# A gated mix of two linear-attention blocks: the gate weights on GpSimd's DMA queue, their transpose moved ahead of x's first block, and one weight load cut in two

## The chip, the core and the metric

The kernel runs on one core of a Trainium2 chip. The metric is the device time in microseconds of one execution; for the kernel before it is the median of three runs, 183.4 us. One further execution was taken by the hardware profiler; its own time was 183.47 us, of which 181.8 us lie between the first and the last instruction (the span). All durations below come from that execution.

The engines are named as in the profile: PE is TensorE (matmuls), PEld its weight loads, DVE is VectorE, ACT is ScalarE, POOL is GpSimd and SP is SyncE, which issues most of the DMAs. A row that ends in "q" after the engine's name (SPq, ACTq, POOLq) is an instruction of that engine's sequencer, such as the issue of a DMA.

## What is computed

One input x of 2048 rows and 640 columns goes through two attention blocks A and B that have weights of their own, and a gate mixes the two results row by row:

```python
x = A_x
g = sigmoid((x * gate_w).sum(-1, keepdims=True))       # gate_w: 640 values
def block(x, wqkv, wo):                                # 32 heads of 20 columns
    q, k, v = split(x @ wqkv)
    phi = lambda t: where(t > 0, t + 1, exp(t)) + 1e-6
    pq, pk = phi(q), phi(k)
    kv = einsum("bhsd,bhse->bhde", pk, v)
    z = einsum("bhsd->bhd", pk)
    num = einsum("bhqd,bhde->bhqe", pq, kv)
    den = einsum("bhqd,bhd->bhq", pq, z)[..., None] + 1e-6
    return heads_together(num / den) @ wo
return g * block(x, A_wqkv, A_wo) + (1 - g) * block(x, B_wqkv, B_wo)
```

## The kernel before

**Tiling.** The 2048 rows of x are 16 chunks of 128 rows; four chunks make a block of 512 rows. The 640 columns are five slabs of 128 (`DT` = 5, index c). Matmuls contract over the columns of x, so x is needed transposed: `xT` holds slab c in its partitions. For x's first block of four chunks, PE transposes the natural rows `xn` (line 250, five transposes of 128x128 a chunk, one for each slab) and DVE copies the result from PSUM to `xT` in two pieces of two and three slabs (line 253). The other three blocks are transposed by the DMA engines (line 172, fifteen DMAs on SP's queue).

**Order.** The body of the program stands in a manually scheduled region: each engine executes its instructions in the order in which the Python code emits them, and waits only for what it reads or overwrites. The stages are: the K projection of A with the gate logits (`k_first`, `k_chunk`), A's Q projection, A's products G = xT times pk and M, then the same for B interleaved with A's late work, then the outer products and the output. What matters here is the start and one load in the middle.

**The loads at the start (lines 157 to 174).** x's first four chunks (`load_x`, 160 KB each) and A's K weights (`load_wk`: slabs 0, 1 and 2 of 160 KB each, then slabs 3 and 4 together, 320 KB) are spread over SP's and ACT's queues. In the order of the code: x chunk 0 on SP, x chunk 1 on ACT, K slab 0 on SP, K slab 1 on ACT, the gate weights `g5` on SP (line 161; five rows of 128 values, 1.2 KB), x chunk 2 on ACT, K slab 2 on SP, x chunk 3 on ACT, K slabs 3 and 4 on SP. Behind them SP issues A's Q weights (line 169, three DMAs) and the fifteen DMA transposes. The framework gives the DMAs of SP and ACT eight completion semaphores in turn; the ninth such DMA uses the first one's semaphore again, and its issuing queue waits until the first has landed. In the kernel before, the ninth is the load of K slabs 3 and 4 on SP; it waits for x chunk 1.

**POOL at the start (lines 177 to 201).** POOL first builds the identity `ident` (a memset and an affine select), which the transposes on PE use, and between and after that the masks and helper matrices `maskE`, `I4`, `spread`, `E4` (a half of the tile `zE`) and a float32 identity in the memory of `GT`.

**The first matmuls.** Seven matmuls on constants (lines 207 to 209) into the PSUM tile `warm_raw` keep PE busy until x arrives. Then `k_first` (line 316) runs:

```python
x_transpose(0, 3)
x_transpose(1, 1)
gate_column(warm_raw)
pts += [ps("kA", 2), ps("kA", 3)]
for hf in range(2):
    for i in range(2):
        part(i, (0, 1), (hf,))
x_transpose(2, 0)
```

`x_transpose(i, slot)` issues the five transposes and two copies of chunk i. `gate_column` (line 220) transposes `g5` on PE into five columns of `warm_raw`'s PSUM slot, and ACT copies them (line 225, three copies) into column 640 of `wk[0]`, A's K weights. So each K matmul of the second half (`hf` = 1) has 321 columns rather than 320, and its last column is the gate's logit. `part(i, (0, 1), (hf,))` is two matmuls of chunk i with slabs 0 and 1 (line 295). The first four K matmuls have `hf` = 0 and do not read the gate column; the next four do.

**The load in the middle.** `Masks` (line 1020) runs A's product `kv_mm` with the V weights of A on PE, and then issues the load of B's V weights, `wvB` (line 1025, 800 KB, through `load_w`, line 864), which takes the memory of A's V weights. `wvB` is first read by the second `kv_mm`, at the first K-V product of B (line 1063).

Of the kernel before, what the change touches and what calls it, by code (L numbers as in the profile page):

```python
# [9 lines left out]
P = 128  # L10
# [7 lines left out]
DT = D // P  # L18
# [15 lines left out]
def kernel(  # L34
# [11 lines left out]
    nc = tc.nc  # L46
# [29 lines left out]
    def ps_raw(name, slot=None):  # L76

        if slot is None:
            slot = turn[0]
            turn[0] = (slot + 1) % 4  # L80
        return pools.get(slot, pools["ps"]).tile([P, 4 * HB], BF16, tag=f"ps{slot}", name=name)
# [5 lines left out]
    def ps(name, slot=None):  # L87

        return banks(ps_raw(name, slot))
# [20 lines left out]
    g5 = persist.tile([DT, P], BF16, name="g5")  # L110
# [37 lines left out]
    wv = [None, None]  # L148
    wq = [None, None]
    wk[0] = wpool.tile([P, DT, D + 2], BF16, tag="wk", name="wkA")  # L150
    def load_x(eng, lo, hi):
        eng.dma_start(out=xn[:, lo:hi, :], in_=xb0[:, lo:hi, :])

    def load_wk(eng, lo, hi):
        eng.dma_start(out=wk[0][:, lo:hi, 0:D], in_=wq_dram[0][:, lo:hi, D:2 * D])

    load_x(nc.sync, 0, 1)
    load_x(nc.scalar, 1, 2)
    load_wk(nc.sync, 0, 1)
    load_wk(nc.scalar, 1, 2)  # L160
    nc.sync.dma_start(out=g5[:], in_=gate_w.rearrange("(c p) -> c p", p=P))
    load_x(nc.scalar, 2, 3)
    load_wk(nc.sync, 2, 3)
    load_x(nc.scalar, 3, 4)
# [5 lines left out]
    for n in range(1, NB):  # L170
        for c in range(DT):
            nc.sync.dma_start_transpose(
                out=xT[:, c, n * HB:(n + 1) * HB], in_=x2[n * HB:(n + 1) * HB, c * P:(c + 1) * P]
# [4 lines left out]
    for r in range(4):  # L178
# [3 lines left out]
        out=spread[:].rearrange("p (h t) -> p h t", t=TW), in_=I4[:, :, None].to_broadcast([P, H, TW])  # L182
    )
    nc.gpsimd.memset(maskE[:], 1.0)
    for lo in range(0, HF, K6):
        part = maskE[:, lo:min(lo + K6, HF)]
        for sign, base in ((1, 0), (-1, Dh - 1)):
            nc.gpsimd.affine_select(
                out=part, in_=part, pattern=[[-sign * Dh, part.shape[1] // Dh], [0, Dh]],
# [3 lines left out]
    for rows, n in ((slice(0, 2 * H), H // 2), (slice(2 * H, P), H)):  # L193
        nc.gpsimd.tensor_copy(
            out=E4_rows[rows, 0:n], in_=I4[rows, 0:n, None].to_broadcast([rows.stop - rows.start, n, Dh])
# [9 lines left out]
    warm_raw = ps_raw("warm", 0)  # L205
# [14 lines left out]
    def gate_column(pt):  # L220

        at = slice(4 * HB - 2 * P, 4 * HB - 2 * P + DT)
        nc.tensor.transpose(out=pt[:, at], in_=g5[:], identity=ident[0:DT, 0:DT])
        for lo, hi in ((0, 1), (1, 2), (2, DT)):
            nc.scalar.copy(out=wk[0][:, lo:hi, D:D + 1], in_=pt[:, at, None][:, lo:hi])
# [21 lines left out]
    def x_transpose(i, slot):  # L247
        pt = ps_raw("xt", slot)
        for c in range(DT):
            nc.tensor.transpose(out=pt[:, c * P:(c + 1) * P], in_=xn[:, i, c * P:(c + 1) * P], identity=ident[:])  # L250
        src = pt[:, 0:D].rearrange("p (c n) -> p c n", c=DT)
        for lo, hi in ((0, 2), (2, DT)):
            nc.vector.tensor_copy(out=xT[:, lo:hi, i * P:(i + 1) * P], in_=src[:, lo:hi])  # L253

    class Phi:

        def __init__(self, dst, src, lifted=False):
            self.dst, self.src, self.lifted = dst, src, lifted
            e = work.tile([P] + list(dst.shape[1:]), BF16, tag="e", name="e", bufs=4)
            self.e = e[:]  # L260
            self.parts = parts = [(self.e, dst, src)] if not isinstance(src, list) else [
                (self.e[:, n], dst[:, n], part) for n, part in enumerate(src)]
            for to, lifted_to, part in parts:
                nc.scalar.activation(out=to, in_=part, func=ACT.Exp)  # L264
                if lifted is True:
                    self.lift(lifted_to, part)
# [26 lines left out]
    def k_mm(b, i, c, pt, hf):  # L293
        n = HF + (b == 0 and hf == 1)
        nc.tensor.matmul(  # L295
            pt[:, hf, 0:n], lhsT=xT[:, c, i * P:(i + 1) * P], rhs=wk[b][:, c, hf * HF:hf * HF + n],
            start=(c == 0), stop=(c == DT - 1),
        )

    def k_done(b, i, pt, lifted=False, between=None):  # L300
        f = Phi(pk[:, i, :].rearrange("p (b n) -> p b n", b=2), pt[:, :, 0:HF], lifted)
        if b == 0:
            nc.scalar.activation(out=gl[:, i:i + 1], in_=pt[:, 1, HF:HF + 1], func=ACT.Exp)
        f.clamp()
        if between is not None:
            between()
        f.top()

    def k_chunk(b, i, slot=None, lifted=False, between=None):
        pt = ps(f"k{'AB'[b]}", slot)  # L310
        for hf in range(2):
            for c in range(DT):
                k_mm(b, i, c, pt, hf)
        k_done(b, i, pt, lifted, between)

    def k_first():

        pts = []

        def part(i, cs, hfs=(0, 1)):  # L320
            for c in cs:
                for hf in hfs:
                    k_mm(0, i, c, pts[i], hf)

        x_transpose(0, 3)
        x_transpose(1, 1)
        gate_column(warm_raw)
        pts += [ps("kA", 2), ps("kA", 3)]
        for hf in range(2):
            for i in range(2):  # L330
# [3 lines that stand above are left out]
            part(i, (2,))  # L334
        x_transpose(3, 1)
        pts.append(ps("kA", 0))
        part(2, (0, 1, 2))
        for i in range(3):
            part(i, (3, 4))
            k_done(0, i, pts[i])  # L340
        k_chunk(0, 3, 1)
# [281 lines left out]
    def kv_mm(b, banks, gs, cs=range(DT)):  # L623

        for g in gs:
            hf, n = g // 3, rows_in(g)
            part = slice(blocks[g].start - hf * HF, blocks[g].stop - hf * HF)
            for k, c in enumerate(cs):
                nc.tensor.matmul(
                    banks[hf][:n, part], lhsT=wv[b][:, c, blocks[g]], rhs=GT[hf][:, c, part],  # L630
                    start=(k == 0), stop=(k == DT - 1),
                )
# [46 lines left out]
    def cells(pt):  # L679
        return [pt[:, hf] for hf in range(2)]  # L680
# [183 lines left out]
    def load_w(b, which, eng, cuts=(0, DT)):  # L864
        lo = {"q": 0, "k": D, "v": 2 * D}[which]
        t = wpool.tile([P, DT, D], BF16, tag="w" + which, name=f"w{which}{'AB'[b]}")
        for c0, c1 in zip(cuts, cuts[1:]):
            eng.dma_start(out=t[:, c0:c1], in_=wq_dram[b][:, c0:c1, lo:lo + D])
        return t
# [76 lines left out]

    with tc.manual_schedule():
        k_first()
        turn[0] = 2
        for n in range(2):  # L950
# [8 lines left out]
        for n in range(1, NB):  # L959
            nc.sync.dma_start(  # L960
                out=xn[:, n * CB:(n + 1) * CB, :], in_=x2[n * HB:(n + 1) * HB, :].rearrange("(q p) d -> p q d", p=P)
# [58 lines left out]
        class Masks:  # L1020

            def __init__(self, slot):
                self.pt = ps("kvA", slot)
                kv_mm(0, cells(self.pt), (0, 1, 2, 3, 5, 4))
                wv[1] = load_w(1, "v", nc.sync)

            def clamp(self):
                kv_mask(0, cells(self.pt), 0, 2)
# [97 lines left out]
        for i in range(1, half):  # L1126
            p, after = pairs[i], pairs[i + 1] if i + 1 < half else None
# [49 lines left out]
```

## Time and profile before

| | |
|---|---|
| median of 3 runs (lowest, highest) | 183.4 us (183.33, 183.84) |
| profiled execution: time, span | 183.47 us, 181.8 us |
| PE busy | 177.5 us |
| DVE, ACT, POOL busy | 148.2, 108.2, 5.5 us |
| DMA moved | 18.85 MB |

In the profile a row of the timeline is "start, duration, engine, line, operation, out<-in, count", and the bracket names how long the engine had been idle before it and who ended that. A PE row's duration is longer than the time to the next one's start, since matmuls are pipelined; for a group of equal matmuls the pitch is (duration of the group minus duration of one) divided by the count less one. The DMA view gives for each issue its size and the time from the start of the issue to the landing. A row of the windows view gives the busy time of each engine in a stretch, the granted clock of PE, the busy share of the DMA engines, and the GB/s.

### The profile page before, as it was taken

What the parts mean: (1) busy time and instruction counts of PE and PEld (TensorE: products, weight loads), DVE (VectorE), ACT (ScalarE), POOL (GpSimd) and SP (SyncE); (2) the same over time, 40 slices, a digit from 0 to 9 for tenths busy, and PEclk for the clock granted to TensorE, in tenths of its full rate; (3) what the DMA queues carried; (4) which work ended last, traced back from release to release, by engine and by line L of the source; (5) the groups of instructions that cost most, each with busy time, mean ns of one, the idle gap of its engine ahead of it and who ended that gap; (6) DMA issues with size and microseconds to landing.
All of it is one profiled execution on the core that took longest, in us unless ns stands there. A gap on an engine that the chain in (4) does not pass through costs nothing.

```text
span 181.8 us, 3375 instructions
## 1 busy us (share of the span) xinstructions
PE 177.5 (98%) x1275; PEld 118.8 (65%) x1285; DVE 148.2 (82%) x267; ACT 108.2 (60%) x210; POOL 5.5 (3%) x23
## 2 busy tenths in 40 slices
PE   7999999999999999999999999999999999999993
PEld 3766656655666677676666665766678777777772
DVE  0478988999999796799898987997988988686764
ACT  2066579976884512785868696964814755466210
POOL 8300000000000000000000000000000000000000
PEclk9999999999999999999999999999999999999999
DMA  5996449984108133005000000053901470222132
GB/s 180 290 177 82 98 103 272 362 176 132 51 4 235 65 116 119 0 0 180 4 2 0 0 4 2 8 149 79 291 17 28 158 180 0 108 88 97 72 130 90
DMA packets 21519, 18.85 MB, mean 104 GB/s; under 512 B 9183, under 2 KB 20991, under 8 KB 21503
## 3 DMA queue, kind: packets, MB, share of 16 engines
q1 hardware_dynamic: 20638, 17.82, 36.1%
q10 hardware_dynamic: 864, 0.82, 1.5%
q8 instruction: 10, 0.16, 0.4%
q14 instruction: 7, 0.05, 0.1%
HBM read 11.86 MB, written 4.80 MB: 92 GB/s over the span
## 4 chain that ended last, share of the span: by engine, by line
PE 96%; DMA 2%; DVE 1%; issue 0%
PE gs L515 17%; PE kA L295 12%; PE kB L295 12%; PE q L413 11%; PE qA L348 7%; PE oy L762 6%; PE oz L762 5%; PE ox L762 4%; PE ow L762 4%; PE q L348 2%; PE gB L485 2%; PE gA L485 2%; DMA xn<-in_A_x_dram 2%; PE qB L348 1%; PE xt L250 1%; PE mA L645 1%
## 5 line engine op out<-in xcount | busy, mean ns | idle before, releaser
L295 PEld LDWEIGHTS <-xT 128*128 128x128 bf16 x320 | 31.1, 98 | 15.0 <-DVE xT L253 0.2
L272 DVE TENSOR_SCALAR e<-e 128x640 bf16<-128x640 bf16 (+2 forms) x58 | 19.6, 339 | 5.8 <-ACT e L264 5.2
L295 PE MATMUL kB<-wkB,xT 128*128 128x320 bf16 x160 | 24.2, 299 | 0.0
L295 PE MATMUL kA<-wkA,xT 128*128 128x320 bf16 (+1 forms) x160 | 23.4, 301 | 0.1
L264 ACT ACTIVATE e<-q 128x512 bf16<-128x512 f32 x26 | 15.7, 603 | 5.0 <-PE q L413 3.9
L515 PEld LDWEIGHTS <-xn 128*128 128x128 bf16 x128 | 12.2, 98 | 6.0 <-issue 1.3
L264 ACT ACTIVATE e<-kB 128x640 bf16<-128x640 f32 x16 | 11.4, 710 | 7.5 <-PE kB L295 7.3
L264 ACT ACTIVATE e<-kA 128x640 bf16<-128x640 f32 x16 | 11.3, 713 | 7.6 <-PE kA L295 7.5
L348 PE MATMUL qA<-xT,wqA 128*128 128x512 bf16 x57 | 13.3, 379 | 0.2
L348 PEld LDWEIGHTS <-wqA 128*128 128x128 bf16 x64 | 7.5, 117 | 5.9
L283 DVE SCALAR_TENSOR_TENSOR pk<-kB,e 128x640 bf16<-128x640 f32 x12 | 9.9, 823 | 1.0
L825 ACT COPY u<-ox 128x320 f32<-128x320 f32 x8 | 3.4, 425 | 11.4 <-PE ox L762 11.4
L762 PEld LDWEIGHTS <-xT 128*128 128x128 bf16 x85 | 8.1, 98 | 2.9
L762 PEld LDWEIGHTS <-pqTA 128*128 128x128 bf16 x85 | 8.1, 98 | 2.8
L767 DVE TENSOR_TENSOR osb<-oz,u 128x320 bf16<-128x320 f32 (+2 forms) x18 | 8.0, 454 | 2.2 <-PE oz L762 1.8
L762 PEld LDWEIGHTS <-pqTB 128*128 128x128 bf16 x80 | 7.8, 98 | 3.0
L515 PE MATMUL gs<-pk,xn 128*128 128x320 bf16 x64 | 9.4, 299 | 0.0
L283 DVE SCALAR_TENSOR_TENSOR pk<-kA,e 128x640 bf16<-128x640 f32 x10 | 8.2, 823 | 0.9
L431 DVE TENSOR_TENSOR q<-q,p 128x512 f32<-128x512 f32 x12 | 8.3, 692 | 0.8 <-PE q L413 0.6
L264 ACT ACTIVATE e<-qA 128x1024 bf16<-128x1024 f32 x6 | 6.2, 1027 | 4.2 <-PE qA L348 3.9
L485 PEld LDWEIGHTS <-xn 128*128 128x128 bf16 x64 | 6.3, 98 | 3.0
L515 PEld LDWEIGHTS <-S 128*128 128x128 bf16 x64 | 6.0, 98 | 2.5 <-issue 0.3
(187 smaller groups left out, 348.2 us busy)
## 6 DMA issues: line engine op xcount, KB each, us to landing
out_dram<-osb SPq DMA_DIRECT2D x14, 160.0 KB, 1.8
xn<-in_A_x_dram SPq DMA_DIRECT2D x3, 640.0 KB, 5.7
wvA<-in_A_wqkv_dram SPq DMA_DIRECT2D x1, 800.0 KB, 10.5
wkB<-in_B_wqkv_dram SPq DMA_DIRECT2D x1, 800.0 KB, 4.7
wqB<-in_B_wqkv_dram SPq DMA_DIRECT2D x1, 800.0 KB, 6.4
wvB<-in_B_wqkv_dram SPq DMA_DIRECT2D x1, 800.0 KB, 4.7
MA<-m_rows SPq DMA_DIRECT2D x1, 800.0 KB, 5.1
MB<-m_rows SPq DMA_DIRECT2D x2, 400.0 KB, 4.2
```

The costliest lines, as they stand in the source:

```text
L264: nc.scalar.activation(out=to, in_=part, func=ACT.Exp)
L272: nc.vector.tensor_scalar(self.e, self.e, 1.0, EPS, op0=ALU.min, op1=ALU.add)
L283: nc.vector.scalar_tensor_tensor(out=dst, in0=src, scalar=1.0 + EPS, in1=e, op0=ALU.add, op1=ALU.max)
L295: nc.tensor.matmul(pt[:, hf, 0:n], lhsT=xT[:, c, i * P:(i + 1) * P], rhs=wk[b][:, c, hf * HF:hf * HF + n], start=(c == 0), stop=(c == DT - 1),
L348: nc.tensor.matmul(dst, lhsT=mixed(wq[b][:, c, :], m), rhs=xT[:, c, n * HB:(n + 1) * HB], start=first, stop=last,)
L413: nc.tensor.matmul(dst, lhsT=left(c), rhs=right(c), start=first and k == 0, stop=k == len(cs) - 1, skip_group_check=not first,)
L431: nc.vector.tensor_tensor(out=dst, in0=src, in1=sb, op=ALU.add)
L485: nc.tensor.matmul(pt[:, hf, 0:HF], lhsT=xn[:, i, c * P:(c + 1) * P], rhs=pk[:, i, hf * HF:(hf + 1) * HF], start=(i == 0), stop=(i == ST - 1),
L515: nc.tensor.matmul(pt[:, n, 0:HF], lhsT=left[:, i, n * P:(n + 1) * P], rhs=right[:, i, :], start=(first and i == 0), stop=(i == hc - 1), s ...
L762: nc.tensor.matmul(dst, lhsT=left[:, c, r0:r0 + P], rhs=right[:, c, :], start=(first and c == 0), stop=(c == DT - 1), skip_group_check=not ...
L767: nc.vector.tensor_tensor(out=dst, in0=acc, in1=sb, op=ALU.add)
L825: nc.scalar.copy(out=self.u2[:], in_=self.at("x"))
```

## The change

Three edits, all that the diff holds:

```diff
+    nc.gpsimd.dma_start(out=g5[:], in_=gate_w.rearrange("(c p) -> c p", p=P))
     load_x(nc.sync, 0, 1)
     load_x(nc.scalar, 1, 2)
     load_wk(nc.sync, 0, 1)
     load_wk(nc.scalar, 1, 2)
-    nc.sync.dma_start(out=g5[:], in_=gate_w.rearrange("(c p) -> c p", p=P))
     load_x(nc.scalar, 2, 3)
     load_wk(nc.sync, 2, 3)
...
+        gate_column(warm_raw)
         x_transpose(0, 3)
         x_transpose(1, 1)
-        gate_column(warm_raw)
         pts += [ps("kA", 2), ps("kA", 3)]
...
                 kv_mm(0, cells(self.pt), (0, 1, 2, 3, 5, 4))
-                wv[1] = load_w(1, "v", nc.sync)
+                wv[1] = load_w(1, "v", nc.sync, (0, 2, DT))
```

The load of the gate weights leaves SP's queue and becomes the first instruction of POOL's own program, in front of the memset that begins `ident`. On PE the gate's transpose stands in front of x's first ten transposes instead of behind them. B's V weights come in two DMAs on SP's queue, slabs 0 and 1, then slabs 2 to 4. Since POOL's DMA counts on a semaphore of its own, the eight semaphores of SP and ACT reach one DMA further: the load of K slabs 3 and 4 is now the eighth and waits for none, A's first Q load is the ninth, and every later DMA of SP up to `wvB` moves one place in the turn. Instructions are otherwise the same on every engine.

## The prediction

> **What bounds the kernel now.** First the page's busy times, then the first piece of the chain of waits that ended last and its shares by engine, then the longest wait of PE's weight loads behind 5.8 us.
>
> ```profile
> PE 177.5 (98%) x1275; PEld 118.8 (65%) x1285; DVE 148.2 (82%) x267; ACT 108.2 (60%) x210; POOL 5.5 (3%) x23
> 0.81 3.06 DMA xn<-in_A_x_dram
> PE 96%; DMA 2%; DVE 1%; issue 0%
> PEld L515 <- issue: 1.6, 5, 0.4
> ```
>
> PE is busy for 98% of the span, and the chain starts with a DMA, the load of x's chunk 0, which lands at 0.81 + 3.06 = 3.87 us. Behind it the chain is PE (96% of the span), but for the last sums on DVE. The longest waits of the weight loads behind 5.8 us, at line 515, are 1.6 us in five places, at most 0.4 each, and no view has PE wait for a DMA there. So a change at the start moves the end only by what it moves the moment from which PE runs without a pause, and a load in the middle moves it only by being late.
>
> That moment is read from the timeline of PE, its weight loads, DVE and ACT in the first 9 us:
>
> ```profile
> 0.84 2.93 PE L209 MATMUL warm<-const-bfloat16-1.0 128*128 128x512 bf16 x7 [0.84 <-PEq L1161]
> 3.92 1.25 PE L250 MATMUL xt<-ident,xn 128*128 128x128 bf16 x10
> 5.10 0.18 PE L223 MATMUL warm<-ident,g 5*128 5x5 bf16 x1
> 5.21 0.71 PE L295 MATMUL kA<-wkA,xT 128*128 128x320 bf16 x2
> 5.55 0.88 PEld L295 LDWEIGHTS <-xT 128*128 128x128 bf16 x6 [0.21 <-DVE xT L253]
> 5.72 0.50 PE L295 MATMUL kA<-wkA,xT 128*128 128x320 bf16 x2
> 6.60 0.44 PE L250 MATMUL xt<-ident,xn 128*128 128x128 bf16 x5
> 4.67 0.29 DVE L253 COPY xT<-xt 128x256 bf16<-128x256 bf16 x1 [3.68 <-PE xt L250]
> 5.20 0.29 DVE L253 COPY xT<-xt 128x256 bf16<-128x256 bf16 x1
> 5.32 0.30 ACT L225 COPY wkA<-warm 128x1 bf16<-128x1 bf16 x3 [1.36 <-PE warm L223]
> ```
>
> PE idles from 3.77 (end of the matmuls on constants) to 3.92. It then issues ten transposes, the gate's transpose at 5.10, the first K matmul of chunk 0 at 5.21 and, after a wait for DVE's third copy (5.20 to 5.49), the first of chunk 1 at 5.72. PE runs slowly there: ten transposes have a pitch of (1.25 - 0.31) / 9 = 0.10 us, five at 6.60 one of (0.44 - 0.22) / 4 = 0.055 us (0.31 and 0.22 are the durations of one). The columns of the granted clock say 1.00 in all these stretches, but the pitch halves between 5.5 and 6 us.
>
> **Gate transpose out of the way (the gain).** Behind the last of the ten transposes, issued at about 4.85, the gate's takes the slots up to 5.21. Without it the first K matmul is free when PE is, at 4.85 + 0.10 = 4.95, and when the first copy is done: 4.67 + 0.29 = 4.96, and 0.06 us more for the signal (DVE's third copy ends at 5.49, the weight load that waits for it starts at 5.55). That gives 5.02, 0.19 us earlier. The second K matmul follows one slow pitch later (0.71 less one duration, 0.24 to 0.27 us), at 5.29; the third needs the third copy, which the gate never held up, and so starts at 5.56 and not at 5.72: 0.16 us won. The last part of this is lost again as long as PE's half rate ends at the same moment: what is done earlier is then done at half rate, so some 0.10 us stays; if the half rate had ended before, all 0.19 would. Floor and ceiling of this term are 0.05 and 0.25 us (the whole 5.21 - 4.95); I take 0.12. ACT's three copies of the gate column move up with the transpose and are needed only by the fifth K matmul.
>
> **Gate weights through POOL (the price).** In front of ten transposes now stands an instruction that waits for g. Queued behind it on PE is everything, with DVE waiting for the transposes and ACT for the K matmuls. No transfer by POOL is in the trace, so its landing is bounded by others:
>
> ```profile
> g<-in_gate_w_dram SPq DMA_DIRECT2D x1, 1.2 KB
> xn<-in_A_x_dram ACTq DMA_DIRECT2D x1, 160.0 KB, 2.9
> xn<-in_A_x_dram ACTq DMA_DIRECT2D x1, 160.0 KB, 4.4
> g_rows<-gr SPq DMA_DIRECT2D x1, 16.0 KB, 1.4
> 1.00:2.00 1.00, 1.00 (x3) 0.29 (x2) 0.00 (x0) 0.00 (x0) 0.97 (x5) 1.00 0.17 28
> 2.00:3.00 1.00, 1.00 (x4) 0.36 (x3) 0.00 (x0) 0.33 (x1) 0.88 (x5) 1.00 0.90 250
> ```
>
> The DMA view has no landing for g before. POOL would issue at 0.80, where its first row of the program stands now. Lower bound: 1.4 us, a small store on free queues, so 2.2 us. Upper bound: 4.4 us, the slowest of the first loads (x chunk 3), so 5.2 us. The nearest are the loads issued at the same moment: x chunk 1 took 2.9 us with 160 KB, and the share of the DMA engines (0.17 in the second microsecond, 0.90 in the third) puts their first packets at about 1.8, one microsecond after the issue. For 1.2 KB I take about that one microsecond, as long again to land, and 0.7 us for POOL to prepare it, over twice what its short instructions below last (0.20 and 0.29): 0.80 + 2.0 + 0.7 = 3.5 us. That is 0.37 us ahead of x chunk 0 at 3.87, so PE transposes the gate in the pause that it has anyway, and the price is nothing. If that cover is gone, each microsecond behind 3.87 costs PE up to one.
>
> [...]
>
> **POOL's own queue.** [...]
>
> ```profile
> 0.80 0.20 POOL masks.py:197 MEMSET ident<- 128x128 bf16 x1 [0.29 <-POOLq L1161]
> 1.34 0.29 POOL masks.py:199 TENSOR_SCALAR_AFFINE_SELECT ident<-ident 128x128 bf16<-128x128 bf16 x1
> 6.19 0.29 POOL masks.py:199 TENSOR_SCALAR_AFFINE_SELECT GT<-GT 128x128 f32<-128x128 f32 x1
> L237 PE MATMUL gt<-GT,gf x1: 272/272/272, 51.6 to 51.6; 128*32 128x128 f32 x1
> ```
>
> `ident` is ready at 1.63 and needed at about 3.8: 2.2 us of cover. The last helper, the float32 identity, is done at 6.48 and first read at 51.6 us. A slip of 0.7 us, or of 2, costs nothing; above 2.2 us it costs one for one.
>
> **SP's queue.** SP loses one issue and one wait:
>
> ```profile
> 1.75 0.37 SPq L161 DMA_DIRECT2D g<-in_gate_w_dram  x1
> 2.17 0.35 SPq L155 DMA_DIRECT2D wkA<-in_A_wqkv_dram  x1
> 3.69 0.39 SPq L155 DMA_DIRECT2D wkA<-in_A_wqkv_dram  x1
> SPq L155 <- DMA xn<-in_A_x_dram: 1.2, 1, 1.2
> wkA<-in_A_wqkv_dram SPq DMA_DIRECT2D x1, 160.0 KB, 4.3
> wkA<-in_A_wqkv_dram SPq DMA_DIRECT2D x1, 320.0 KB, 4.0
> 2.19 0.45 ACTq L152 DMA_DIRECT2D xn<-in_A_x_dram  x1
> 6.88 0.71 PE L295 MATMUL kA<-wkA,xT 128*128 128x320 bf16 x4
> 7.43 0.44 PE L250 MATMUL xt<-ident,xn 128*128 128x128 bf16 x5
> ```
>
> K slab 2 is issued at 1.75 instead of 2.17, slabs 3 and 4 at about 2.2 instead of 3.69 (the 1.2 us wait for x goes to the first Q load behind it), and the Q loads and DMA transposes come some 0.5 us earlier. None of this is worth time: slab 2 lands at 2.17 + 4.3 = 6.5 and is read at 6.88, slabs 3 and 4 land at 7.7 and are read five transposes and six matmuls behind 7.43, at 8.5, and PE waits for neither. Nor should it cost any. The DMA engines are nearly full from 2 us on (0.90), and SP's loads run one behind the other, so an earlier issue mostly waits longer. If slabs 3 and 4 did get ahead of x chunk 3 (lands at 2.19 + 4.4 = 6.6, needed at 7.43), it could be 320 KB / 250 GB/s = 1.3 us late, and PE would wait 0.5 us.
>
> The tightest landing behind that is the last DMA transpose of block 1:
>
> ```profile
> 11.20 1.26 SPq L172 DMA_TRANSPOSE xT<-in_A_x_dram  x1
> xT<-in_A_x_dram SPq DMA_TRANSPOSE x1, 4.8
> 15.86 1.25 PE L295 MATMUL kA<-wkA,xT 128*128 128x320 bf16 x8
> ```
>
> It lands at 16.0; slab 4 is read as the fifth matmul, 15.86 + 4 x 0.136 = 16.4 us (pitch (1.25 - 0.30) / 7). PE comes 0.12 us earlier, the issue 0.5: the 0.4 us of slack stay.
>
> **B's V weights in two.** One more issue of about 0.37 us on SP, where the queue is empty, and the same bytes.
>
> ```profile
> 81.84 0.37 SPq L868 DMA_DIRECT2D wvB<-in_B_wqkv_dram  x1
> wvB<-in_B_wqkv_dram SPq DMA_DIRECT2D x1, 800.0 KB, 4.7
> L629 PE MATMUL kvB<-GT,wvB x15: 199/218/218, 136.5 to 137.2; 128*120 128x120 bf16 x10, 128*80 128x80 bf16 x5
> 117.10 4.29 SPq L654 DMA_DIRECT2D m_rows<-MA  x5
> ```
>
> The load lands at 86.5 and is read at 136.5; SP's next issue is at 117.1. Cost and gain are nothing, even if the second half took twice as long.
>
> **Sum.** 183.47 of the profiled execution less 0.12 is 183.35; it lies 0.07 above the median of the runs shown, so the forecast against the median is 183.3 us, no change that a measurement can tell (0.3% is 0.55 us, the bound used below).
>
> **Rivals.** (1) g comes late. It decides from a landing at 3.87 on, place the gate's wait on PE. For: the path of POOL is unseen here, the DMA engines fill up from 2 us, and the bound reaches 5.2. Against: 1.2 KB on a ring of its own need not stand behind 160 KB loads as on SP. At the bound the loss is 5.2 - 3.87 + 0.1 for the gate itself less 0.12: 184.7 us. Slower by over 0.55 us begins near a landing of 4.5.
>
> (2) The pause also keeps PE slow. The pitch halves at about 5.8, 5 us after PE's first matmul; if a longer pause puts that off, work runs at half rate for longer. Until now a pause of 0.15 us did not matter; nothing shows what one of 1 us does. [...] From the rows: if the half rate lasted as long again as it did behind 3.92 (1.9 us), half of that, 0.95, comes on top of rival 1, 185.6 us.
>
> (3) Better than the sum: the half rate ends earlier, or both the whole 0.25 and a run's scatter (lowest 183.33) fall together; 182.8 us would need another 0.4 us, and no row has such a wait to remove: the only idle times of PE ahead of 6 us are 0.15 and 0.21.
>
> (4) The edits do nothing: g in time, but K's first matmul held by something else at 5.21. That is 183.4, inside the forecast's own band.
>
> **How the numbers follow.** Forecast with (4), within 0.55 us: 0.64. This includes g up to 0.6 us late. Rivals 1 and 2, slower by more: 0.26, of which 0.06 for the half rate. Rival 3, faster by more: 0.10. The forecast's own range is 183.1 to 183.9; eight in ten with half of rival 1 and a part of rival 3: 182.9 to 184.5.
>
> **What would show it.** In the profile after: the gate's transpose ahead of 3.92 and the ten transposes still released by x's DMA (sum right), or released by g's at a later time (rival 1; that time less 3.92 is its price); the third K matmul near 5.56; five transposes at a pitch of 0.055 near 6.5 (rival 2 if it is 0.10); POOL's identity finished before 3.8; PE waiting for no K weights, no x chunk 3 and no xT. A difference that arises behind 17 us would make the whole working wrong.

## The result, and the profile after

The changed kernel takes 185.37 us (median of 12 runs, 184.08 to 185.94); the kernel before, run beside it, 183.63 us (12 runs, 183.26 to 183.88). The ratio is 1.0085, 95% interval 1.0067 to 1.0104: slower, by some 1.6 us, and its median lies 0.9 us above 184.5, the upper end of the range that the prediction gave eight chances in ten.

The 12 runs fall into two groups with a gap between them: three at 184.08 to 184.16 and nine at 185.20 to 185.94. The execution that was profiled is one of the first group (184.08 us). So this profile shows one part of the loss and hides the other.

The start of PE in the profile after, from its timeline:

```profile
0.85 2.93 PE L209 MATMUL warm<-const-bfloat16-1.0 128*128 128x512 bf16 x7 [0.85 <-PEq L1161]
4.92 0.17 PE L223 MATMUL warm<-ident,g 5*128 5x5 bf16 x1 [1.13 <-DMA g<-in_gate_w_dram]
5.02 0.73 PE L250 MATMUL xt<-ident,xn 128*128 128x128 bf16 x10
5.86 1.46 PE L295 MATMUL kA<-wkA,xT 128*128 128x320 bf16 x8
7.15 0.44 PE L250 MATMUL xt<-ident,xn 128*128 128x128 bf16 x5
```

PE stands still for 1.13 us, from 3.78 to 4.92, until g lands; x's ten transposes start at 5.02 instead of 3.92. Yet the transposes of x's chunk 2 come only 0.55 us later than before (7.15 against 6.60), because in this execution PE already ran at its full rate when x came: the ten transposes have a pitch of (0.73 - 0.22) / 9 = 0.057 us, where the execution of before had 0.10. The shift stays near that: A's Q projection begins 0.56 us later than before, the first K-V product of B (below) 0.6, and the span is 0.6 us longer.

POOL's timeline and the DMA view say why g was late:

```profile
1.29 0.64 POOL L157 DMA_DIRECT2D g<-in_gate_w_dram  x1 [0.78 <-POOLq L1161]
2.48 0.31 POOL masks.py:199 TENSOR_SCALAR_AFFINE_SELECT ident<-ident 128x128 bf16<-128x128 bf16 x1
g<-in_gate_w_dram POOLq DMA_DIRECT2D x1, 1.2 KB, 3.6
```

POOL starts on the transfer at 1.29, not at 0.80, works 0.64 us on it, and g lands 3.6 us after 1.29, at 4.9. The identity is complete at 2.79 us, a slip of 1.16, and holds up nothing.

The other loads of the start moved too. From the DMA view and SP's timeline, x's chunks 2 and 3 (issued on ACT at 1.75 and about 2.2), then the load of K slabs 3 and 4:

```profile
xn<-in_A_x_dram ACTq DMA_DIRECT2D x1, 160.0 KB, 4.5
xn<-in_A_x_dram ACTq DMA_DIRECT2D x1, 160.0 KB, 5.1
2.21 0.43 SPq L155 DMA_DIRECT2D wkA<-in_A_wqkv_dram  x1
wkA<-in_A_wqkv_dram SPq DMA_DIRECT2D x1, 320.0 KB, 5.3
```

Slabs 3 and 4 are issued at 2.21 (before: 3.69) and land at 7.5 (before: 7.7), hardly sooner; x's chunks land at 6.3 and 7.3, 0.9 and 0.7 us later than before (there 3.6 and 4.4 us after their issue). In this kernel PE does not reach them before 7.15 and 7.98, so it does not wait. (The first DMA in the turn of semaphores is x's chunk 1 on ACT in both kernels; in the changed one A's first Q load, now the ninth, waits for it and goes out at 3.88.)

B's V weights in two transfers land in 3.1 and 4.0 us, issued at 82.4 and 82.8 us, and are read at 137.1, as the view of that tile says:

```profile
L629 PE MATMUL kvB<-GT,wvB x15: 199/218/218, 137.1 to 137.8; 128*120 128x120 bf16 x10, 128*80 128x80 bf16 x5
L868 SPq DMA_DIRECT2D wvB<-in_B_wqkv_dram x2: 373/418/463, 82.4 to 82.8; - x2
```

### The profile page after: what moved, and what is told of

The parts are those of the page before. It is cut to its first block, busy times and chain, and to the rows that moved or that the text cites. A ratio compares the mean times of both kernels' runs of the same rounds, so it can differ in the third digit from the quotient of the medians.

```text
span 182.4 us, 3388 instructions
## 1 busy us (share of the span) xinstructions
PE 177.4 (97%) x1285; PEld 118.2 (65%) x1285; DVE 148.2 (81%) x267; ACT 108.2 (59%) x210; POOL 6.1 (3%) x24
## 4 chain that ended last, share of the span: by engine, by line
PE 95%; DMA 2%; DVE 1%; issue 0%; POOLq 0%
PE gs L515 17%; PE kA L295 12%; PE kB L295 12%; PE q L413 11%; PE qA L348 7%; PE oy L762 6%; PE oz L762 5%; PE ox L762 4%; PE ow L762 4%; PE q L348 3%; PE gB L485 2%; PE gA L485 2%; DMA g<-in_gate_w_dram 2%; PE qB L348 1%; PE mA L645 1%; PE kvA L629 1%
```

## The experiments

The theory after the result: the loss is PE's pause in front of x, which costs twice, as lost time and by putting off the moment from which PE runs at its full rate. The rivals: POOL's queue, or the shifted turn of SP's semaphores, costs by itself. Medians are compared with runs of the kernel before on the same chip in the same series (183.10, 183.39, 183.14 and 183.35 us in the four series).

### Each edit alone

**e1_queue_only** has the first line of the diff (g by POOL, none by SP) and nothing else.

> The kernel before with only the gate's load moved to POOL's queue; its transpose stays behind x's ten transposes. Theory (the loss is the wait of PE in front of x): g lands again at about 4.9 us, needed only at 4.95 to 5.1, so no pause: 183.4 to 183.9, same as before, all runs within 0.6 us. Rival (POOL's queue or the shifted turn of SP's semaphores cost time by themselves): 184.1 or more.

Measured: 183.85 us (183.55 to 184.15), ratio 1.0033 (1.0019 to 1.0048). The time lies in the theory's band, but the kernel before took 183.10 us in this series: a third of a per cent is lost although PE does not pause in front of x. The profile shows one new wait of PE, for x's chunk 3:

```profile
3.76 1.25 PE L250 MATMUL xt<-ident,xn 128*128 128x128 bf16 x10
7.49 0.28 PEld L250 LDWEIGHTS <-xn 128*128 128x128 bf16 x5 [0.22 <-DMA xn<-in_A_x_dram]
```

It is taken up again below.

**e2_order_only** has the second edit alone; g stays on SP:

```diff
+        gate_column(warm_raw)
         x_transpose(0, 3)
         x_transpose(1, 1)
-        gate_column(warm_raw)
```

> The kernel before with only the gate's transpose moved in front; g stays third on SP's queue, where it landed at about 4.8 us. Theory: PE pauses from 3.8 to 4.8 as in the changed kernel, and the time is as there: 184.1 in some runs, 185.2 to 185.9 in most, median 185.0 to 185.6. Rival (POOL's path is what costs): 183.4 to 184.0.

Measured: 185.19 us (183.71 to 185.67), ratio 1.0098 (1.0064 to 1.0131), the whole loss of the changed kernel. So with g on SP the order alone costs as much. Its profile is of an execution of 185.65 us, and PE's timeline shows the second cost:

```profile
4.41 0.18 PE L223 MATMUL warm<-ident,g 5*128 5x5 bf16 x1 [0.63 <-DMA g<-in_gate_w_dram]
4.52 1.25 PE L250 MATMUL xt<-ident,xn 128*128 128x128 bf16 x10
5.62 2.32 PE L295 MATMUL kA<-wkA,xT 128*128 128x320 bf16 x8
8.27 1.28 PE L295 MATMUL kA<-wkA,xT 128*128 128x320 bf16 x4
9.86 1.40 PE L295 MATMUL kA<-wkA,xT 128*128 128x320 bf16 x9
```

The pause is only 0.63 us. But eight K matmuls take 2.32 us, where in the profile of before they took 1.55:

```profile
5.21 1.55 PE L295 MATMUL kA<-wkA,xT 128*128 128x320 bf16 x8
```

In e2 four at 8.27 still have a pitch near 0.27 us (1.28 less one duration, 0.47, by 3); from 9.86 on it is (1.40 - 0.30) / 8 = 0.14. PE ran at half rate until nearly 9.8 us, in the execution of before until 5.8. The column of the granted clock (the last but two in the windows view) does not show it:

```profile
6.50:7.50 1.00, 1.00 (x6) 0.53 (x5) 0.00 (x0) 0.00 (x0) 0.00 (x0) 1.00 0.97 264
```

The other two profiles of executions above 185.3 us, those of e5 and e14 below, have the half rate until about 9.7 and 8.2 us; the profiles of the changed kernel near 184.0 us have the full rate from x's first transpose on (ten in 0.73 us).

**e3_wv_only** has the third edit alone.

> The kernel before with only B's V weights in two transfers. Theory and prediction: no effect, 183.3 to 183.9. Rival (the second issue or the extra wait costs something): over 184.0.

Measured: 183.08 us, ratio 1.0003 (0.9985 to 1.0020). No effect.

### The pause and the rate, apart

**e4_filled** and **e10_filled_less** are the changed kernel with the pause filled by matmuls on constants, so that PE is never idle but g is as late as ever; **e12_after_again** is the changed kernel in the series of e10.

```diff
-    for n in [HB] * 6 + [RB]:
+    for n in [HB] * 9 + [RB]:         # e4
+    for n in [HB] * 8 + [RB] * 2:     # e10
```

> The changed kernel with three more matmuls of 512 columns on constants, which fill PE's pause until about 5.05 us at PE's first rate. Theory (two costs: the pause itself, and a later doubling of PE's rate because of the pause): the second cost goes, the first stays, all runs 184.0 to 184.4, no runs above 184.8. Rival (the spread of the changed kernel comes from g landing at different times): the spread stays, median 185.2 to 185.6. Third (PE's rate does not matter, only the wait): same median as the changed kernel.

> The changed kernel with two more matmuls of 512 and one of 256 columns on constants, so the filling ends at about 4.85 us, just ahead of g. Theory (pause: a direct cost of about 1.1 us, and a part that comes from PE's rate): all runs within 0.8 us of each other, median 0.2 to 0.6 us above the lowest, 1.0 to 1.3 us above before, and 0.3 to 0.9 us below the changed kernel on the same chip. Rival (filling changes nothing but the spread is chance): same median and spread as the changed kernel.

> The changed kernel once more, on the same chip as e10_filled_less and e11_no_load, to compare with them: 0.7% to 1.0% above before, with runs in two groups, some 0.5 to 0.9 us and some 1.7 to 2.4 us above before.

Measured: e4 184.47 us (184.15 to 184.91), ratio 1.0067 (1.0044 to 1.0090); e10 184.46 us (184.08 to 184.70), ratio 1.0068 (1.0052 to 1.0084); the changed kernel again 185.51 us (184.02 to 185.79), ratio 1.0105 (1.0074 to 1.0136), two runs of its six at 184.0 to 184.3 and four at 185.3 to 185.8. The filled kernels have no run above 185 us, though e4's highest, 184.91, lies above the 184.8 that the theory allowed; in e10's series the median falls by 1.05 us, more than I expected. PE's timeline in e10:

```profile
0.85 4.00 PE L209 MATMUL warm<-const-bfloat16-1.0 128*128 128x512 bf16 x10 [0.85 <-PEq L1161]
4.92 0.17 PE L223 MATMUL warm<-ident,g 5*128 5x5 bf16 x1
5.03 0.73 PE L250 MATMUL xt<-ident,xn 128*128 128x128 bf16 x10
```

The gate's transpose is exactly where it is in the changed kernel. What the filling takes away comes from the idle PE. What is left with PE busy, 0.68% or 1.25 us, is put down to the late start of x; it still holds some of the rate, since in e4's profile (184.50 us) PE has x's ten transposes at half rate (1.25 us for the ten, as in the profile of before) although it was never idle:

```profile
5.11 1.25 PE L250 MATMUL xt<-ident,xn 128*128 128x128 bf16 x10
```

**e6_before_pause** makes the idle PE without anything late: the kernel before with four matmuls on constants instead of seven.

```diff
-    for n in [HB] * 6 + [RB]:
+    for n in [HB] * 4:
```

> The kernel before with four matmuls on constants instead of seven, so PE has nothing to do from about 2.55 to 3.9 us; x and g are as before. [...] Rival (only the late start costs, the rate does not depend on the pause): 182.9 to 183.6.

Measured: 184.42 us (184.07 to 185.48), ratio 1.0053 (1.0034 to 1.0072). The rival, at most 183.6 us, fell. The edit moves no load and takes away nothing but three matmuls on constants, and the kernel is 1.0 us longer. (PE's pause and the smaller number of matmuls ahead of x come together here; the run does not part them.) Its PE timeline:

```profile
3.84 1.25 PE L250 MATMUL xt<-ident,xn 128*128 128x128 bf16 x10 [1.13 <-DMA xn<-in_A_x_dram]
5.13 2.25 PE L295 MATMUL kA<-wkA,xT 128*128 128x320 bf16 x8
7.21 0.44 PE L250 MATMUL xt<-ident,xn 128*128 128x128 bf16 x5
```

x is on time (3.84), the K matmuls start at 5.13, and still the eight take 2.25 us; PE's rate doubles about a microsecond later than before in this execution.

### g in time

**e5_early_act** puts g at the head of ACT's queue, its transpose in front as in the changed kernel.

```diff
-    nc.gpsimd.dma_start(out=g5[:], in_=gate_w.rearrange("(c p) -> c p", p=P))
+    nc.scalar.dma_start(out=g5[:], in_=gate_w.rearrange("(c p) -> c p", p=P))
     load_x(nc.sync, 0, 1)
```

> The changed kernel, but g is the first DMA on ACT's queue (the loads of ACT move back by one issue, some 0.4 us) instead of POOL's; its transpose stays in front of x's. Theory (all of the loss is g's landing behind x's chunk 0): g lands at 3.0 to 3.8, PE has no pause beyond x's own landing, and the time is 182.8 to 183.4, same as before or 0.1 to 0.3 us less, with no runs above 184. Rival (a transpose in front of x is costly in itself, or ACT's later loads of x and K weights now stall PE): 183.8 or more.

Measured: 185.07 us (184.24 to 185.84), ratio 1.0083 (1.0052 to 1.0115). The rival holds. From PE's timeline and its weight loads:

```profile
3.71 0.18 PE L223 MATMUL warm<-ident,g 5*128 5x5 bf16 x1
3.82 1.37 PE L250 MATMUL xt<-ident,xn 128*128 128x128 bf16 x10
5.85 2.03 PE L295 MATMUL kA<-wkA,xT 128*128 128x320 bf16 x7 [0.40 <-DMA wkA<-in_A_wqkv_dram]
7.47 0.68 PEld L250 LDWEIGHTS <-xn 128*128 128x128 bf16 x5 [0.18 <-DMA xn<-in_A_x_dram]
8.21 1.27 PE L295 MATMUL kA<-wkA,xT 128*128 128x320 bf16 x4
```

g is no longer waited for, but K slab 1, third on ACT's queue now, is: the remaining seven of the first eight K matmuls wait until 5.85. Here the place at the head of the queue was paid for by the loads behind it: K slab 1 lands at 1.80 + 4.0 = 5.8 us, before at 1.22 + 3.3 = 4.5. The waits are short, but this execution (185.68 us) is again one at half rate, until about 9.7 us (pitch 0.27 at 8.21), with PE never idle for more than 0.40 us at a time behind its first matmul on constants. In e5 too SP has lost the DMA of g, and K slabs 3 and 4 go out at 2.20 us, so the run does not tell these causes apart.

**e7_quiet_pool** measures POOL's path where the DMA engines are quiet: the store of the gate's rows at 52 us goes by POOL.

```diff
-        nc.sync.dma_start(out=g_rows[:], in_=rows[:])
+        nc.gpsimd.dma_start(out=g_rows[:], in_=rows[:])
```

> The kernel before with another DMA moved from SP to POOL: the store of the gate's rows at about 52 us, 16 KB, on nearly idle DMA engines; on SP it took 1.4 us from issue to landing. It measures POOL's path without the traffic of the start. Theory (POOL's path is slow by itself): 2.5 to 3.6 us to the landing. Rival (the 3.6 us of g at the start are the full DMA engines): 1.6 to 2.2 us. The time of the kernel stays at 182.9 to 183.6 in either case, since what reads these rows waits until about 61 us.

Measured: 183.57 us, ratio 1.0004 (0.9982 to 1.0026). The path, from POOL's timeline and the DMA view:

```profile
52.05 0.62 POOL L240 DMA_DIRECT2D g_rows<-gr  x1 [45.55 <-ACT gr L239]
g_rows<-gr POOLq DMA_DIRECT2D x1, 16.0 KB, 1.8
```

1.8 us to the landing, 1.4 by SP: the path itself costs 0.4 us here, and it was this kernel's first DMA by POOL as well. It is a store of 16 KB and not a load of 1.2 KB, so the other 1.8 us of g's 3.6 are not measured by it alone. The semaphores' records in the traces help: the same 1.2 KB landed 1.4 us after its issue at the head of ACT's queue (e5, at 2.16 us, ahead of the big loads), and 2.6 to 3.1 us after its issue on SP at about 1.75 us, behind the first of them (ten profiles, e2's row below among them, where PE had it at 4.41). So most of the delay belongs to the moment and not to POOL. That it is the full engines (busy share in the third microsecond 0.90 before, 0.84 after) is argued; no run emptied them at that moment.

```profile
1.73 0.36 SPq L161 DMA_DIRECT2D g<-in_gate_w_dram  x1
```

**e11_no_load** takes the load away: a constant stands in the tile of the gate weights, so the gate's logits are not computed; the transpose stays in front.

```diff
-    nc.gpsimd.dma_start(out=g5[:], in_=gate_w.rearrange("(c p) -> c p", p=P))
+    nc.vector.memset(g5[:], 0.03)
```

> The changed kernel without the load of the gate weights: a memset on DVE at the start fills their tile with a constant, so the gate's transpose stands in front of x and waits for no DMA; the gate's logits are then not the reference's. This is the order alone, with g in time. Theory (all of the loss is the wait for g): 0.1 to 0.5 us less than before. Rival (the transpose in front costs in itself): at or above before.

Measured: 184.56 us (183.62 to 185.02), ratio 1.0066 (1.0041 to 1.0091). The theory fell: with no wait for g, the kernel is still slower. Its weight loads on PE and its DMA view show a new wait:

```profile
7.12 0.28 PEld L250 LDWEIGHTS <-xn 128*128 128x128 bf16 x5 [1.40 <-DMA xn<-in_A_x_dram]
8.19 0.28 PEld L250 LDWEIGHTS <-xn 128*128 128x128 bf16 x5 [0.40 <-DMA xn<-in_A_x_dram]
xn<-in_A_x_dram ACTq DMA_DIRECT2D x1, 160.0 KB, 5.3
xn<-in_A_x_dram ACTq DMA_DIRECT2D x1, 160.0 KB, 5.9
wkA<-in_A_wqkv_dram SPq DMA_DIRECT2D x1, 320.0 KB, 6.2
```

PE waits for x's chunks 2 and 3, which land 5.3 and 5.9 us after their issue; before it was 3.6 and 4.4.

### The transpose later, and SP's turn

**e8_between** leaves g on SP and moves the transpose back; **e9_between_pool** does the same with g on POOL (both have B's V weights in one transfer).

```diff
-        gate_column(warm_raw)
...
-        for hf in range(2):
-            for i in range(2):
-                part(i, (0, 1), (hf,))
+        part(0, (0, 1), (0,))
+        gate_column(warm_raw)
+        part(1, (0, 1), (0,))
+        for i in range(2):
+            part(i, (0, 1), (1,))
```

> The kernel before with the gate's transpose moved back instead of forward: behind the first two K matmuls (chunk 0, slabs 0 and 1, first half) and ahead of chunk 1's; g stays on SP. Theory (PE has room there, while chunk 1 waits for DVE's copy, and the first K matmul no longer stands behind the gate): 0.1 to 0.4 us less than before, 182.7 to 183.0 where before is 183.1. Rival (the gate column now comes too late for the second half, and PE waits for ACT's copies): 183.2 to 183.6.

> g on POOL's queue as in the changed kernel, its transpose behind the first two K matmuls as in e8_between; one transfer of B's V weights. Theory (POOL's load costs only because PE needs g before it has landed at about 4.9 us): here it is needed at about 5.3 to 5.7, so the time is that of before within 0.3%, as e8_between. Rival (POOL's path or the shifted turn of SP's semaphores costs by itself): 0.3% or more above before, as e1_queue_only.

Measured: e8 183.57 us, ratio 0.9999 (0.9978 to 1.0020), no gain; e9 184.07 us (183.87 to 184.90), ratio 1.0060 (1.0039 to 1.0081). In e9 g has landed before it is read, so the loss has another cause, as its rival had it. The weight loads of its profile wait where e11's did, for x's chunk 3:

```profile
7.78 0.28 PEld L250 LDWEIGHTS <-xn 128*128 128x128 bf16 x5 [0.39 <-DMA xn<-in_A_x_dram]
```

What e1, e9 and e11 share with the changed kernel, and e8 does not, is the removed DMA on SP: K slabs 3 and 4 go out without waiting for x's chunk 1, and K slab 2 some 0.4 us earlier. The last four kernels give that place in SP's turn back, with a load of 1.2 KB into a tile that nobody reads.

```diff
     load_wk(nc.scalar, 1, 2)
+    nc.sync.dma_start(out=g5x[:], in_=gate_w.rearrange("(c p) -> c p", p=P))
     load_x(nc.scalar, 2, 3)
```

**e13_no_load_turn** is e11 with it (the gate's logits are left out there too), **e14_after_turn** the changed kernel, **e15_queue_turn** e1 and **e16_between_pool_turn** e9.

> e11_no_load (constant gate weights, transpose in front of x) with a load of the gate weights into an unused tile at g's old place on SP, which restores SP's turn. Theory (the earlier load of K slabs 3 and 4 delays x's chunks 2 and 3): chunk 2 lands again at about 5.4, chunk 3 at 6.6, PE does not wait, and the time is 0.1 to 0.5 us below before. Rival (the transpose in front costs in itself): 0.5% or more above before, as e11_no_load.

> The changed kernel with SP's turn restored in the same way. Theory (in the changed kernel the wait for g hides the late chunks of x): no better than the changed kernel by more than 0.3 us: 0.7 to 1.1% above before, again in two groups of runs. Rival (the late chunks of x make half of its loss): 0.3 to 0.5% above before.

> e1_queue_only (g on POOL, transpose in its old place) with SP's turn restored. e1_queue_only was 0.33% over before. Theory (both causes share it: g at 4.9 us, needed at 4.4 to 5.1, and chunk 3 of x): about half remains, 0.1 to 0.3% over before. Rival (g alone): 0.3 to 0.4%; rival (turn alone): 0.0 to 0.1%.

> e9_between_pool (g on POOL, transpose behind the first two K matmuls) with SP's turn restored. e9_between_pool was 0.6% over before. Theory (all of that is the late chunks of x): the time of before within 0.15%, as e8_between. Rival (POOL's path costs by itself): 0.4% or more above before.

| kernel | without the place | with it (ratio to before) |
|---|---|---|
| constant gate weights, transpose in front (e11, e13) | 1.0066 (1.0041 to 1.0091) | 1.0012 (1.0000 to 1.0023) |
| g on POOL, old order (e1, e15) | 1.0033 (1.0019 to 1.0048) | 1.0001 (0.9987 to 1.0016) |
| g on POOL, transpose later (e9, e16) | 1.0060 (1.0039 to 1.0081) | 1.0010 (0.9999 to 1.0021) |
| changed kernel (after, e14) | 1.0085 (1.0067 to 1.0104) | 1.0098 (1.0059 to 1.0136) |

With the place given back x's chunk 3 is early again, as the DMA view of e9 (first line) and e16 shows:

```profile
xn<-in_A_x_dram ACTq DMA_DIRECT2D x1, 160.0 KB, 5.5
xn<-in_A_x_dram ACTq DMA_DIRECT2D x1, 160.0 KB, 4.3
```

So it is in every profile: 3.8 to 4.7 us from its issue to its landing in the ten in which K slabs 3 and 4 wait, 5.1 to 5.9 in the seven in which they do not (e5 left aside, where chunk 3 itself is held). The place also puts K slab 2 back by 0.4 us; no run parts the two loads.

The loss goes in the first three, all but about 0.1%; in e1 all of it, and I had expected half. PE's waits for x's chunk 3 in the profiles of e1 and e9, 0.22 and 0.39 us, are less than the losses, 0.6 and 1.1 us; where the rest arises is open. In the changed kernel it stays: there PE is held for g so long that late chunks of x are not felt, and its profile has no wait for them. (The interval of e14 leaves room for some 0.4% either way.) Its profile, of an execution of 185.37 us, has half rate until about 8.2 us:

```profile
6.14 2.31 PE L297 MATMUL kA<-wkA,xT 128*128 128x320 bf16 x8
```

Two losses lie one behind the other, and only the first is paid.

In e13 the transpose in front waits for no g and SP's order is as before, and still nothing is gained, where the theory had 0.1 to 0.5 us. PE's timeline shows where a gain would go:

```profile
3.71 0.18 PE L225 MATMUL warm<-ident,g 5*128 5x5 bf16 x1
5.06 1.45 PE L297 MATMUL kA<-wkA,xT 128*128 128x320 bf16 x8
8.62 0.57 PE L297 MATMUL kA<-wkA,xT 128*128 128x320 bf16 x3 [0.17 <-DMA wkA<-in_A_wqkv_dram]
```

The K matmuls start 0.15 us earlier than before, and at 8.62 PE meets the load of slabs 3 and 4, which in this execution landed at 8.6 us (before: 7.7). That this is what holds the kernel is argued from one profile. No version that ran is faster than the kernel before.

## Why the prediction was wrong, step by step

- **What bounds the kernel.** Held. PE is 97% busy after, and every loss that was located lies in the first 10 us.
- **Gate weights through POOL (the price).** This step failed. I took g's landing at 3.5 us, ahead of x's chunk 0, within bounds of 2.2 and 5.2, and priced the wait at nothing; g landed at 4.87, and PE stood still for 1.13 us. The bounds held, the choice did not. The sum was 0.80 for the start, 0.7 for POOL's own work on the transfer and 2.0 to the landing; measured are 1.29, 0.64 and 2.94 us. POOL began 0.5 us late, for a reason that no run shows, and I let one microsecond pass from the first packets to the landing, where x's own loads took two. On quiet engines e7 measured POOL's path at 0.4 us more than SP's (1.8 us against 1.4). Rival 1's formula gives 4.87 - 3.87 + 0.1 - 0.12 = 1.0 us for this landing; e10 has 1.25 us (0.95 to 1.54 by its interval), and the three lowest runs of the changed kernel lost only 0.5 (the profiled one among them had PE at its full rate when x came).
- **Rival 2, PE's rate.** Right in its effect, too small a chance (0.06), and it carries the median out of the range: rival 1's formula alone gives 183.4 + 1.0 = 184.4 us, still inside. Two thirds to three quarters of the changed kernel's runs (4 of 6, 9 of 12) are in the upper group, 1.0 to 1.9 us above the lower one. e6 shows an early pause, with three matmuls fewer, to cost although nothing is late, e4 and e10 the upper group gone with the pause, and the profiles of e2, e5 and e14 the late doubling. The sign that I had named, a pitch of 0.10 in the five transposes near 6.5, is absent from the profile after (0.055 at 7.15), because that execution is of the lower group. From the rows I had let the half rate last 1.9 us longer; in e2 it lasts until 9.8 us, four microseconds longer than before. The medians of the two groups are 1.3 us apart (184.13 and 185.47). Why one kernel has two groups, no run shows.
- **SP's queue.** "Nor should it cost any" failed. With the earlier issue x's chunk 3 lands later in every profile (5.1 to 5.9 us after its issue against 3.8 to 4.7; that the slabs take the DMA engines from it is argued, the loss and its going are shown), and giving the place back wins 0.3 to 0.5% where PE reaches the chunks in time. The wait that I had bounded at 0.5 us was the right one for chunk 3 (0.22 to 0.40 us in e1, e9 and e11); that chunk 2 could come late too, as in e11 (1.40 us), I had not considered. No part of it shows in the changed kernel itself (e14).
- **Gate transpose out of the way (the gain).** I took 0.12 us, 0.05 to 0.25; e13 measures a loss of 0 to 0.4 us (its ratio's interval by 183.35 us), so no gain. The first K matmul does start earlier; in e13's profile PE then meets K slabs 3 and 4.
- **POOL's own queue; B's V weights.** Held: the identity slipped 1.16 us of 2.2, and e3 gives 1.0003.

## What to carry to other kernels

A small load that the first matmul waits for has to be priced at the landing it can have among the loads of the start (here 3.6 us for 1.2 KB), not at its size; put its consumer where the slack is and not in front of what is on the path. Removing a DMA from a queue whose completion semaphores are used in turn changes when later DMAs go out (here K slabs 3 and 4 at 2.21 us and not at 3.69), and an accidental wait can be what keeps a big load behind the small ones that are needed first (x's chunk 3 landed 3.8 to 4.7 us after its issue with the wait, 5.1 to 5.9 without). When a change pauses PE early, compare the groups of runs and not one profile: here the pause had a price of its own in PE's rate, and matmuls on constants showed how much of the loss that was (1.05 us of the median in e10's series).

## What the hardware showed that I had not expected

A DMA of 1.2 KB issued by POOL at the start landed 3.4 to 3.8 us after POOL began on it in nine profiles, 16 KB on quiet engines in 1.8. With a pause of PE of only 0.63 us behind three microseconds of matmuls, the profile of e2 has half rate until about 9.8 us, and e5's, with pauses of at most 0.40 us, until about 9.7, while the column of the granted clock stays at 1.00 in these stretches. And in the changed kernel an issue 1.5 us earlier brought 320 KB in only 0.2 us sooner, while two loads of 160 KB came 0.7 to 0.9 us later.
